# Layer A of the second chunk in other buffers, with newly searched engine orders

## The chip, the cores and the metric

One core of a Trainium2 chip runs the whole program. Its engines work side by side and wait for each other by semaphores: TensorE (PE, matmuls; its weight loads are shown as PEld), VectorE (DVE), ScalarE (ACT) and GpSimd (POOL); SyncE (SP) issues nearly all of the DMA transfers. The metric is the time of one execution in device microseconds, the median of some runs.

## The reference

Four layers are applied to x of shape 2048 x 512: A, B, A, B, each as x + layer(layernorm(x)). Both kinds have 32 heads of 16. In layer A a position sees 8 positions, two apart, back to 14; in layer B it sees the last 256.

```python
def _A_ref(x, wqkv, wo):                      # H = 32, Dh = 16, W, dil = 8, 2
    idx = pos[:, None] - off[None, :]         # off = arange(W) * dil
    logits = einsum("bhsd,bhswd->bhsw", q, k[idx]) * scale      # masked where idx < 0
    o = einsum("bhsw,bhswd->bhsd", softmax(logits), v[idx])
    return o @ wo
def _B_ref(x, wqkv, wo):
    mask = (idx[:, None] - idx[None, :] >= 0) & (idx[:, None] - idx[None, :] < 256)
    p = softmax(where(mask, einsum("bhqd,bhkd->bhqk", q, k) * Dh ** -0.5, -1e9))
    return einsum("bhqk,bhkd->bhqd", p, v) @ wo
x = x + _A_ref(_layernorm(x), A_wqkv, A_wo);  x = x + _B_ref(_layernorm(x), B_wqkv, B_wo)   # twice
```

## The kernel before

The 2048 positions are cut into 8 chunks of 256. The loop goes over the two pairs of layers and, in each, over the chunks: layer A of a chunk, then layer B of it (16 pairs; A0 and B0 are chunk 0 of the first pair, A1 and B1 chunk 1, and so on to A15 and B15). Numbers of 32 bits that go through the projections are split into a high and a low half of 16 bits ("xh" and "xl", "wB1h" and "wB1l"), and a projection does three matmuls for each block (L1015 to L1017, or L1035, L1037 and L1038).

**Preparing the weights.** `prep` loads the four weight blocks of A and then of B (s = 0, 1, 2 for q, k, v; s = 3 for the output), takes their squares to find a scale (L830, L832), writes the high halves on ACT (L911) and the low halves on DVE (L909, "wB3l", "wB1l" and so on). The blocks of q, k and v are staged in the stk tiles, which layer B later uses for its stacked q and k; their rows of padding are written by transfers (L1562, "stk<-pad") once the staged weights have been read. The output weights are staged in slots of the pool p6 (L799).

**Layer A** (`layer_a`). The norm ends with a scalar computation on DVE, POOL and DVE again (rs, L942, L945, L948); ACT scales the tile (xn, L964), makes the high half (ht, L974), and transfers transpose it (L976, L977). After the projections ACT evicts q (L1131), k and v (L1133). Each chunk needs the last 14 columns of k and v of the chunk before, the halo: POOL copies them to a spare tile (ha, L1140) and into the next chunk's k and v (L1123). Then 16 products of q with shifted k (pr, L1152, on DVE or POOL) are summed on PE (L1160); a softmax on DVE and ACT follows (max L1183, subtraction L1186); its weights are spread on PE (L1229), multiplied with shifted v on DVE (pw, L1242) and summed on POOL (L1249 to L1251) or DVE (L1247). `finish` splits the output (oh L1059, ol L1061), projects it and adds it to the residual (y, L1069), and stores it (L1080).

**Layer B** (`layer_b`). The norm scales the tile on ACT (xn, L986), transposes it on PE (L990), and splits it (xh L995, xl L996). K and Q are projected and evicted as halves (eh L1270, el L1273), written to DRAM (the puts, "re<-eh", "re<-el", L1283) and read back stacked (the stacks, "stk<-re", L1294). The scores are computed once for their maxima (L1336, L1339; DVE L1350 in a first chunk, L1354 and L1358 in the others), the maxima go through DRAM into the stacked q (L1391, L1397), then the scores come again with the maximum subtracted (L1430, L1432), the exponential on ACT (p, L1436), the mask on POOL (L1445), and the product with v (L1462), evicted to os (L1498). The output is gathered into oc, divided and finished like layer A's.

**The pools that the change touches.** po4 has one slot for each of its tags q, oa and ob; pos has two slots "os"; p6 has three. Layer B's output oc is an ob, its evictions are the two os, its exponentials p are p6. Layer A has its q and output in po4's q and oa, and its k and v in two "kv" slots; only layer A of chunk 1 in the first pair is kept elsewhere, since at that time chunk 0 still holds those slots:

```python
if l == 0 and c == 1:
    q, o = (buf("pos", [P, 4, C], F32, "os", f"{n}{l}_{c}") for n in "qo")
    kv = {s: buf("pp6", [P, 4, HALO + C], F32, "p6", f"kv{l}_{c}_{s}") for s in (1, 2)}
```

**The order of the work.** Every step is a task of a plan: `plan.add` names its engine, an assumed duration, what it reads and writes, and for a transfer a size, from which the plan assumes its time. The table ORDER holds a number for each task, by scope (A1, B0, pB for preparing B's weights, W for 110 groups of three idle matmuls that keep PE busy). On each engine the tasks run in the order of their numbers; a negative number sends a task to its other engine (for example a product from DVE to POOL). `Plan.order` then merges the five lists into the order in which the program is written, by the assumed durations and by the slots that are free; the engines themselves wait only for data and slots.

Of the kernel before, what the change touches and what calls it, by code (L numbers as in the profile page):

```python
# [678 lines left out]
def kernel(  # L679
# [420 lines left out]
    def layer_a(l, c):  # L1100
# [119 lines left out]
        for n in range(4):  # L1220
# [11 lines left out]
            for a in range(2):  # L1232
# [21 lines left out]
                plan.add("POOL", 2.56, total, r=[vpw], w=[vr], alt=("DVE", 1.84))  # L1254
        finish(l, c, o, vo)


    def layer_b(l, c):
        d = st8[l, c] = {}
        first = c == 0  # L1260
# [353 lines left out]
```

## Time and profile before

| | us |
|---|---|
| median of 3 runs | 1444.02 |
| lowest, highest | 1441.65, 1450.58 |
| the profiled execution's own time | 1450.06 |
| its span, from the first to the last instruction | 1448.3 |

The profile is of one execution. Its page gives the busy time of each engine and the span in 40 slices of about 36.2 us; the timeline gives each instruction's start, duration, engine, source line, output and inputs, and in brackets how long its engine sat idle before it and what ended that. A stretch of the busy-time view gives, after the stretch's length, the busy time of PE, PEld, DVE, ACT and POOL with the number of instructions in parentheses, then the granted clock of TensorE, the share of the DMA engines that was busy, and GB/s. A row of the waits gives the engine and line that waited, what it waited for, the total in us, how many times, and the longest.

### The profile page before, as it was taken

To read this page: it belongs to the slowest core of one execution; us is meant where nothing else is said; L and a number is where in the kernel's file an instruction comes from. 1 tells how busy PE (TensorE), PEld (TensorE's weight loads), DVE (VectorE), ACT (ScalarE), POOL (GpSimd) and SP (SyncE) were. 2 spreads that over 40 slices of the span, in tenths; PEclk is the share of its full clock that TensorE was granted. 3 is DMA by queue.
4 is the path that set the end of the run, shared out by engine and by line. 5 is a ranking of instruction groups with operands and counts; after the bars stand their busy time and mean duration, and the time that the engine had idled before them with its cause. 6 is when DMAs were issued, how large, how long until landed. Compare 5 with 4: busy or idle time off the path is not lost.

```text
span 1448.3 us, 35229 instructions
## 1 busy us (share of the span) xinstructions
PE 1340.7 (93%) x13918; PEld 782.8 (54%) x13918; DVE 1170.6 (81%) x2254; ACT 732.9 (51%) x1054; POOL 690.3 (48%) x784
## 2 busy tenths in 40 slices
PE   9985989999999998999999898999989999898998
PEld 7651646556364554736456363645637465464554
DVE  7867696996969879697996869698796978969693
ACT  6621345554555455455555434555455555545564
POOL 3445163462846336273563727254272734637232
PEclk9995989999999999999999999999999999999999
DMA  8242223233252323324133233324334242332331
GB/s 244 70 103 58 84 56 117 71 92 97 74 121 75 89 79 87 105 69 112 48 106 106 73 117 76 107 60 99 89 83 119 48 119 54 86 102 73 99 80 53
DMA packets 135943, 130.45 MB, mean 90 GB/s; under 512 B 68448, under 2 KB 94560, under 8 KB 135776
## 3 DMA queue, kind: packets, MB, share of 16 engines
q1 hardware_dynamic: 135520, 127.93, 32.7%
q8 instruction: 109, 1.79, 0.5%
q14 instruction: 58, 0.48, 0.1%
q10 hardware_dynamic: 256, 0.26, 0.1%
HBM read 67.11 MB, written 43.48 MB: 76 GB/s over the span
## 4 chain that ended last, share of the span: by engine, by line
PE 37%; DVE 17%; DMA 5%; issue 4%; SPq 3%; ACT 3%; POOL 2%; DVEq 0%; POOLq 0%; ACTq 0%
PE banks L1015 6%; PE banks L1016 5%; PE banks L1017 5%; PE banks L1462 4%; DVE m L1354 4%; DVE banks L1358 3%; PE banks L1430 3%; PE banks L1160 3%; DVE pw L1242 2%; PE banks L1037 2%; PE banks L1336 2%; PE banks L1035 2%; ACT p L1436 2%; PE banks L1038 2%; PE banks L1339 1%
## 5 line engine op out<-in xcount | busy, mean ns | idle before, releaser
L1436 ACT ACTIVATE p<-banks,sclB 128x768 f32<-128x768 f32 x480 | 418.5, 901 | 290.0 <-PE banks L1432 205.5
L1445 POOL TENSOR_SCALAR_AFFINE_SELECT p<-p 128x1024 f32<-128x1024 f32 x240 | 261.2, 1095 | 344.8 <-ACT p L1436 301.4
L1354 DVE TENSOR_REDUCE m<-banks 128x2 f32<-128x512 f32 x448 | 297.1, 685 | 3.4
L1358 DVE COPY_PREDICATED banks<-maskt,banks 128x256 f32<-128x256 int16 x448 | 179.1, 422 | 67.9 <-PE banks L1339 53.3
L1462 PE MATMUL banks<-p,v 128*32 128x128 f32 (+1 forms) x3840 | 196.8, 333 | 5.8 <-POOL p L1445 4.3
L1152 DVE TENSOR_TENSOR pr<-kv,q 128x512 f32<-128x512 f32 x220 | 153.6, 747 | 32.5 <-PE banks L1160 20.1
L1430 PE MATMUL banks<-stk,stk 64*128 64x256 f16 x960 | 136.3, 285 | 30.4 <-DVE m L1354 12.5
L1462 PEld LDWEIGHTS banks<-p,v 128*32 128x32 f32 x3840 | 106.5, 110 | 101.2 <-issue 34.3
L1242 DVE TENSOR_TENSOR pw<-banks,kv 128x1024 f32<-128x1024 f32 x128 | 152.7, 1214 | 4.2 <-POOL o L1251 2.4
L1339 PE MATMUL banks<-stk,stk 48*128 48x128 f16 (+1 forms) x1024 | 127.3, 252 | 13.1 <-DVE m L1350 9.0
L1249 POOL TENSOR_TENSOR pw<-pw 128x512 f32<-128x512 f32 x100 | 127.2, 1272 | 12.8 <-DVE pw L1242 12.6
L1336 PE MATMUL banks<-stk,stk 48*128 48x128 f16 (+1 forms) x896 | 112.0, 253 | 22.5 <-DVE m L1354 7.9
L1430 PEld LDWEIGHTS <-stk 64*128 64x128 f16 x960 | 57.0, 95 | 117.1 <-issue 108.8
L1432 PE MATMUL banks<-stk,stk 64*128 64x128 f16 x960 | 109.4, 224 | 0.0
L1336 PEld LDWEIGHTS <-stk 48*128 48x128 f16 x896 | 51.1, 95 | 98.1 <-issue 88.5
L1273 DVE SCALAR_TENSOR_TENSOR el<-banks,eh 128x512 f16<-128x512 f32 x64 | 42.4, 684 | 75.1 <-ACT eh L1270 27.4
L1270 ACT ACTIVATE eh<-banks 128x512 f16<-128x512 f32 x64 | 37.3, 596 | 77.8 <-PE banks L1017 42.3
L1250 POOL TENSOR_TENSOR pw<-pw 128x256 f32<-128x256 f32 x100 | 72.8, 728 | 7.8
L1152 POOL TENSOR_TENSOR pr<-kv,q 128x512 f32<-128x512 f32 x36 | 46.2, 1299 | 60.0 <-PE banks L1160 35.5
L1015 PE MATMUL banks<-xh,wA0h 128*128 128x256 f16 x256 | 70.1, 274 | 4.8 <-DMA xh<-ht 1.8
L1160 PE MATMUL banks<-pr,sel 128*32 128x512 f32 x512 | 71.7, 610 | 1.2 <-DVE pr L1152 1.2
L1339 PEld LDWEIGHTS <-stk 48*128 48x128 f16 x1024 | 52.8, 96 | 34.8 <-issue 32.6
(196 smaller groups left out, 3127.8 us busy)
## 6 DMA issues: line engine op xcount, KB each, us to landing
stk<-re SPq DMA_DIRECT2D x256, 96.0 KB
re<-eh SPq DMA_DIRECT2D x128, 128.0 KB
xm<-y SPq DMA_DIRECT2D x32, 256.0 KB
re<-el SPq DMA_DIRECT2D x64, 128.0 KB
y<-xm SPq DMA_DIRECT2D x32, 256.0 KB
oc<-os SPq DMA_DIRECT2D x120, 64.0 KB
os<-scr SPq DMA_DIRECT2D x15, 512.0 KB
x<-in_A_x_dram SPq DMA_DIRECT2D x16, 256.0 KB
```

The source lines that it names most:

```text
L1015: nc.tensor.matmul(ps[mp].t[:, i], wh, xh, start=k == 0, stop=False)
L1152: E.tensor_mul(pr.t, window(kv[1].t, m, 64 * tq, 64)[:, 0], qb)
L1242: nc.vector.tensor_mul(pw.t, pb.t.unsqueeze(1).broadcast_to([P, 2, W, 64]), v)
L1249: E.tensor_add(t[:, :, 0:4], t[:, :, 0:4], t[:, :, 4:8])
L1336: nc.tensor.matmul(ps.t[:, par, 0 : (2 - qb) * P], lhs, stk[hf, bef][r, col, qb * P :], start=True, stop=True)
L1339: nc.tensor.matmul(ps.t[:, par, (2 - qb) * P : 3 * P], lhs, stk[hf, now][r, col, : (1 + qb) * P], start=True, stop=True)
L1354: nc.vector.tensor_reduce(out=m.t[:, :, u, qb], in_=ps.t[:, :, 0 : 2 * P], op=ALU.max, axis=AX.X)
L1358: nc.vector.copy_predicated(t[:, :, 0:P], maskt[:, 0:P].bitcast(I16).unsqueeze(1).broadcast_to([P, 2, P]), t[:, :, 2 * P : 3 * P])
L1430: nc.tensor.matmul(o[:, two], k[:, jf * P : (jf + 1) * P], q, start=True, stop=True)
L1436: nc.scalar.activation(pt.t[:, :, 2 * i : 2 * i + 2].rearrange("p s m q -> p m s q"), ps.t[:, :, : 3 * P].rearrange("p m (s q) -> p m s q" ...
L1445: nc.gpsimd.affine_select(out=v, in_=v, pattern=[[0, 8], [-1 if b == 0 else 1, P]], compare_op=ALU.is_gt if b == 0 else ALU.is_ge, fill=0. ...
L1462: nc.tensor.matmul(o, v[:, jj, 17 * h : 17 * h + 32], rhs, start=z == 0 and (b == 0 or first), stop=z == 1 and b == 1, tile_position=(0, 3 ...
```

## The change

Three things change in the code, and all of ORDER.

The buffers of layer A, chunk 1 of the first pair: q goes to po4's q, the output to po4's ob, k and v to the two os slots. For this the os tiles are made 14 columns longer in each of their four rows, and layer B reaches the part that it uses through a flat view.

```diff
-            q, o = (buf("pos", [P, 4, C], F32, "os", f"{n}{l}_{c}") for n in "qo")
-            kv = {s: buf("pp6", [P, 4, HALO + C], F32, "p6", f"kv{l}_{c}_{s}") for s in (1, 2)}
+            q, o = buf("po4", [P, 4, C], F32, "q", f"q{l}_{c}"), buf("po4", [P, 4, C], F32, "ob", f"o{l}_{c}")
+            kv = {s: buf("pos", [P, 4, HALO + C], F32, "os", f"kv{l}_{c}_{s}") for s in (1, 2)}
...
+    def flat(b):
+        return b.t.rearrange("p g t -> p (g t)")[:, 0 : 4 * C]
...
-            os_[hf] = buf("pos", [P, 4, C], F32, "os", f"os{l}_{c}_{hf}")
+            os_[hf] = buf("pos", [P, 4, HALO + C], F32, "os", f"os{l}_{c}_{hf}")
...
-                nc.scalar.copy(os_[hf].t[:, 2 * hp : 2 * hp + 2], acc.t)
+                nc.scalar.copy(flat(os_[hf]).rearrange("p (g t) -> p g t", g=4)[:, 2 * hp : 2 * hp + 2], acc.t)
```

The other uses of the os tiles (`divide`, `leave`, `gather`, `gather_o`, `spread` and the last multiplication) go through `flat` in the same way.

What the plan assumes of some transfers:

```diff
-                    plan.add("SP", 0.5, lambda j=j, load=load: load(j), w=touched[j], size=512)
+                    plan.add("SP", 0.5, lambda j=j, load=load: load(j), w=touched[j], size=700)
...
-        plan.add("SP", 0.37, lambda: nc.sync.dma_start(xb.t, fetch(t)), r=[after[t]] if after else [], w=[vx], size=300)
+        plan.add("SP", 0.37, lambda: nc.sync.dma_start(xb.t, fetch(t)), r=[after[t]] if after else [], w=[vx], size=350)
...
-                    plan.add("SP", 0.62, put, r=ve[n], w=[vre[par][z]], size=128)
+                    plan.add("SP", 0.64, put, r=ve[n], w=[vre[par][z]], size=128)
...
-                plan.add("SP", 1.23, stack, r=vre[0] + vre[1], w=[vst[hf, i, hp]], size=192)
+                plan.add("SP", 1.3, stack, r=vre[0] + vre[1], w=[vst[hf, i, hp]], size=192)
```

And a new number for every task in ORDER, of which this is the part of scope A1 that holds chunk 1's 16 products (entries 77 to 80, 82 to 85, 87 to 90 and 92 to 95):

```diff
-        188, 191, 192, 54, 56, 22, 37, -27, 101, -26, 98, 217, -32, -30, -29, 111, 241, 116, -34, -33, 115, 245, 117,
-        -37, -36, -35, 255, 122, 123, 68, 125, 126, 127, 69, -40, 262, 138, 42, 134, 40, 263, 136, 41, 135, -140,
+        176, 182, 55, 52, 22, 20, 98, -24, 96, -28, 200, 102, 108, 113, -29, 235, 118, 117, 119, -33, 245, 122, 123,
+        121, 120, 250, 124, 125, 67, 127, 129, 131, 69, -34, 261, 144, 36, 139, 34, 262, 141, 35, 143, -147, 265,
```

Sorted by the new numbers, the engines run the following where the orders around the first layer B differ most (chunk 0 unless chunk 1 is named; j is the half of a weight block):

| | before | after |
|---|---|---|
| DVE, from the last part of layer A to layer B's norm | wB1l (j 0), ol, wB0l (j 1), residual y of tile 0, norm statistics of tile 0, y of tile 1, scale, wB3l (j 1), wB1l (j 1), wB2l (j 1), rest of the norm | wB1l (j 0), ol, wB0l (j 1), wB2l (j 1), both residuals, the whole norm, a scale and one product of chunk 1, wB1l (j 1); wB3l (j 1) after the xl of layer B |
| POOL, up to the norm's rstd (L945) | chunk 0's last sum of layer A; halo into chunk 1's v; spare halo of chunk 1's k; rstd | last sum; spare halo of chunk 1's v; halo into chunk 2's v; spare halo of chunk 1's k; one product of chunk 1; spare halo of chunk 0's v; halo into chunk 1's v; rstd |
| ACT, from the second oh to layer B's first xn | oh, one half of chunk 1's v, xn | oh, other half of v, two weight splits, first half of v, xn |
| PE, chunk 1's v projection | partly after chunk 0's output projection | done among chunk 0's output projection |
| PE, layer B | K, one product sum of chunk 1, Q, V | one product sum of chunk 1, K, one step of V, Q, V |
| SP, ahead of layer B's K puts | pads, a store of y, ht transpose, x load, second store, pads | pads, a store of y, x load, ht transpose, pad, y load, second ht transpose, pads |
| DVE, layer B's first maxima | four of them, then chunk 1's max and subtraction | chunk 1's max and subtraction, then the first of them |
| DVE / POOL, chunk 1's products | 6 / 10 | 12 / 4 |
| DVE / POOL, all products of layers A | 220 / 36 | 235 / 21 |

The number of tasks on each engine: POOL 562 before and 547 after, DVE 2021 and 2032, ACT 1040 and 1044, SP 784 and PE 3560 in both.

More of the change, by code (lines that the diff above doesn't have):

```diff
@@ L1477, in divide @@
                     v = sh.t.rearrange("p (b x) -> p b x", x=32)
-                    r = os_[hf].t[:, 2 * hp : 2 * hp + 2].rearrange("p g t -> p (g t)")
+                    r = flat(os_[hf])[:, 2 * hp * C : 2 * (hp + 1) * C]
                     nc.vector.transpose(sh.t, acc.t.rearrange("p a t -> p (a t)"))
@@ L1484, in leave @@
                 def leave(m0, E, hp=hp, hf=hf):
-                    s_ = os_[hf].t[:, 2 * hp : 2 * hp + 2].rearrange("p g t -> p (g t)")
+                    s_ = flat(os_[hf])[:, 2 * hp * C : 2 * (hp + 1) * C]
                     o_ = o.t[:, 2 * hp : 2 * hp + 2].rearrange("p g t -> p (g t)")
@@ L1510, in gather @@
             def gather(hf=hf):
-                s_ = os_[hf].t.rearrange("p g t -> p (g t)")
+                s_ = flat(os_[hf])
                 for m in range(4):
@@ L1516, in gather_o @@
             def gather_o(hf=hf):
-                s_ = os_[hf].t.rearrange("p g t -> p (g t)")
+                s_ = flat(os_[hf])
                 for m in range(4):
@@ L1528, in spread @@
         def spread():
-            nc.sync.dma_start(os_[1].t.rearrange("p g t -> p (g t)"), scr.t.unsqueeze(0).broadcast_to([16, 8, 4 * C]))
+            nc.sync.dma_start(flat(os_[1]), scr.t.unsqueeze(0).broadcast_to([16, 8, 4 * C]))
         plan.add("SP", 0.55, spread, r=[vscr, *vog], w=[vbc], size=840)
@@ L1536, in layer_b @@
             sl = slice(t * P, (t + 1) * P)
-            plan.add("DVE", 0.61, lambda E, sl=sl: E.tensor_tensor(out=o.t[:, :, sl], in0=o.t[:, :, sl], in1=os_[1].t[:, :, sl], op=ALU.mult),
+            plan.add("DVE", 0.61, lambda E, sl=sl: E.tensor_tensor(out=o.t[:, :, sl], in0=o.t[:, :, sl], in1=flat(os_[1]).rearrange("p (g t) -> p g t", g=4)[:, :, sl], op=ALU.mult),
                      r=[vbc, *vog], w=[v], mode="S", alt=("POOL", 1.3))
```

834 rows, old and new, of the table ORDER are left out of this document.

## The prediction

> **What bounds the kernel now.** I read the page first, then the busy time by stretches, then each engine's timeline over the first 130 us, because the buffers that the change moves are used only there.
>
> ```profile
> span 1448.3 us, 35229 instructions
> ...
> PE 1340.7 (93%) x13918; PEld 782.8 (54%) x13918; DVE 1170.6 (81%) x2254; ACT 732.9 (51%) x1054; POOL 690.3 (48%) x784
> ...
> PE   9985989999999998999999898999989999898998
> ...
> PEclk9995989999999999999999999999999999999999
> ```
>
> TensorE (PE) is busy 93% of the span and VectorE (DVE) 81%. The weak places are slices 3 and 4 (80 to 150 us), where both the PE digits and the clock fall, and some later slices with an 8, such as 23 and 25 (796 to 833 and 869 to 905 us).
>
> ```profile
> 75.00:112.00 37.00, 27.66 (x197) 17.46 (x195) 21.72 (x33) 8.68 (x14) 16.90 (x18) 0.94 0.47 112
> 112.00:150.00 38.00, 25.40 (x140) 7.89 (x140) 33.08 (x104) 6.98 (x11) 20.31 (x24) 0.61 0.19 46
> 150.00:280.00 130.00, 124.45 (x1287) 77.34 (x1286) 103.97 (x220) 63.13 (x93) 50.44 (x58) 0.96 0.32 89
> 280.00:1400.00 1120.00, 1053.67 (x11269) 608.87 (x11267) 926.37 (x1737) 582.20 (x835) 559.47 (x617) 0.97 0.33 88
> ```
>
> From 280 to 1400 us PE is busy 1053.67 of 1120 us: 66.3 us idle, 6%. What is gained before 280 us therefore moves the end by about as much, for everything behind it is PE work that only begins earlier. From 75 to 112 us no engine is full (PE 27.66 of 37, DVE 21.72): a chain of latencies sets the pace. From 112 to 150 us DVE is the bound (33.08 of 38) and the clock is down to 0.61.
>
> **The change part by part.** *The buffers.* Before, layer A of chunk 1 kept k and v in two of the three p6 slots, two of which first hold the staged B output weights.
>
> ```profile
> 77.32 0.70 POOL L1123 COPY kv<-ha 128x56 f32<-128x56 f32 x1 [8.10 <-DVE wB3l L909]
> ...
> 80.98 0.70 POOL L945 TENSOR_TENSOR rs<-rs,mhalf 128x2 f32<-128x2 f32 x1 [2.29 <-DVE rs L942]
> 81.63 0.23 POOL L1123 COPY kv<-ha 128x56 f32<-128x56 f32 x1
> ```
> ```profile
> 64.95 1.12 ACT L911 ACTIVATE wB2h<-stk,pscB 128x1024 f16<-128x1024 f32 x1
> ...
> 71.23 0.60 ACT L1059 CAST oh<-o 128x512 f16<-128x512 f32 x1
> 77.37 0.60 ACT L1133 ACTIVATE kv<-banks 128x512 f32<-128x512 f32 x1 [5.54 <-DVE wB3l L909]
> 81.91 0.81 ACT L986 ACTIVATE xn<-y,rs 128x512 f32<-128x512 f32 x1 [3.94 <-DVE rs L948]
> ...
> 86.03 0.81 ACT L964 ACTIVATE xn<-x,rs 128x512 f32<-128x512 f32 x1
> ...
> 98.58 0.60 ACT L1270 ACTIVATE eh<-banks 128x512 f16<-128x512 f32 x1 [0.39 <-PE banks L1017]
> ...
> 149.56 0.59 ACT L1498 COPY os<-banks 128x512 f32<-128x512 f32 x1 [2.88 <-PE banks L1462]
> ```
>
> GpSimd (POOL) stood 8.10 us before it could write chunk 1's halo, ScalarE (ACT) 5.54 us before it could evict v: both ended by "wB3l", the last read of a staged slot. With k and v in the os slots, which layer B of chunk 0 doesn't fill before its first eviction at 149.56 us, this wait is gone. By itself that is worth nothing on the chain: right after, POOL waits for "DVE rs" until 80.98 and ACT for "DVE rs" until 81.91. Late next is DVE. The other side of the exchange, q in po4's q slot and the output in ob, should wait for nobody: chunk 0's products have long read their q when chunk 1's is evicted, and layer B's own output enters ob only behind that eviction at 149.56.
>
> *DVE's order around the norm of layer B, chunk 0.* This is what the freed slot allows.
>
> ```profile
> 73.82 0.74 DVE L1069 SCALAR_TENSOR_TENSOR y<-banks,sclA,y 128x512 f32<-128x512 f32 x1
> ...
> 75.21 0.73 DVE L1069 SCALAR_TENSOR_TENSOR y<-banks,sclA,y 128x512 f32<-128x512 f32 x1
> ...
> 75.98 1.28 DVE L909 SCALAR_TENSOR_TENSOR wB3l<-stageB,pscB,wB3h 128x1024 f16<-128x1024 f32 x1
> 77.17 1.47 DVE L909 SCALAR_TENSOR_TENSOR wB1l<-stk,pscB,wB1h 128x512 f16<-128x512 f32 x2
> 78.52 1.28 DVE L909 SCALAR_TENSOR_TENSOR wB2l<-stk,pscB,wB2h 128x1024 f16<-128x1024 f32 x1
> ...
> 80.72 0.17 DVE L942 TENSOR_SCALAR rs<-mv 128x2 f32<-128x2 f32 x1
> ```
>
> Before, between the last residual (75.21) and the first norm scalars (80.72) lie wB3l (75.98 to 77.17, 1.19), wB1l (77.17 to 78.52, 1.35), a scale (0.12) and wB2l (1.19). wB3l had to be early, since a slot hung on it. The new numbers put wB3l, wB1l and the scale behind the scalars and wB2l before the first residual. wB2l still counts; the rest is 1.19 + 1.35 + 0.12 = 2.66 us. So the scalars come at about 78.06, and xn on ACT at 79.25 where it was 81.91. On POOL the rstd now has six instructions ahead of it: two halo pairs, a spare halo copy and one product, 5 x 0.23 (the row at 81.63; one at 77.32 took 0.70) and a product of about 1.3 (its row is below), together 2.4 us. They wait for v's last eviction, which ACT does after the second oh (71.23 + 0.60), one other eviction (0.60) and two weight splits (1.12 each), so it ends near 75.3; POOL is free near 77.7, 0.6 us before it's wanted (78.06 + 0.26, as 80.98 stood to 80.72).
>
> *Behind the norm.* PE gets chunk 1's first product sum ahead of K instead of between K and Q, which is neutral for Q, and one step of V (two matmuls, 98.38 to 98.81) ahead of Q:
>
> ```profile
> 98.38 0.38 PE L1037 MATMUL banks<-wB2h,xh 128*128 128x512 f16 x1
> ...
> 98.81 0.38 PE L1035 MATMUL banks<-wB2h,xl 128*128 128x512 f16 x1
> ```
>
> That is +0.43. Q's last high half was evicted at 98.58; it comes 2.66 - 0.43 = 2.2 us earlier. SyncE's queue (SP) gets two transfers moved ahead of the K puts, a transposed ht tile and a y load:
>
> ```profile
> 82.06 1.26 SPq L976 DMA_TRANSPOSE xh<-ht  x1
> 84.71 0.36 SPq L1088 DMA_DIRECT2D x<-in_A_x_dram  x1
> ...
> 88.68 2.54 SPq L1562 DMA_DIRECT2D stk<-pad  x4
> 93.19 2.53 SPq L1283 DMA_DIRECT2D re<-eh  x4
> ...
> 103.39 5.67 SPq L1294 DMA_DIRECT2D stk<-re  x8
> ```
>
> They issue in 1.26 and 0.36 us. The y load also needs a free x slot, which the xn of chunk 2's second tile gives (86.03 + 0.81, now some 2.7 earlier: 84.2), before the pads can go anyway. Queued behind them are the pads of stk and all puts. SP stood idle from 91.22 (88.68 + 2.54) to 93.19, 1.97 us, which hides 1.62; with that cover gone they'd cost 1.6. The stacks then issue near 101.2 instead of 103.39.
>
> *The stretch bound by DVE.*
>
> ```profile
> 112.41 0.42 DVE L1350 CUSTOM_DVE_ANT_0 j<-banks,maskt 128x256 bf16<-128x256 f32 x1 [6.15 <-DMA stk<-pad]
> ...
> 116.04 0.69 DVE L1183 TENSOR_REDUCE mx<-banks 128x64 f32<-128x512 f32 x1
> 116.76 0.69 DVE L1186 TENSOR_TENSOR e<-banks,mx 128x512 f32<-128x512 f32 x1
> ```
>
> Chunk 1's max and subtraction (0.69 each, 1.4 us) stood among layer B's maxima. In the new order they stand ahead of the first of these, in the wait for the stacks (the bracket at 112.41: DVE idle 6.15 us). To be ready in time, chunk 1's products go from 6 on DVE and 10 on POOL to 12 and 4. That takes 1.4 us out of a stretch where DVE is the bound.
>
> *The products elsewhere.* Over the whole kernel 15 more products are on DVE (220 to 235, POOL 36 to 21), 9 of them outside chunk 1.
>
> ```profile
> L1152 DVE TENSOR_TENSOR pr<-kv,q 128x512 f32<-128x512 f32 x220 | 153.6, 747 | 32.5 <-PE banks L1160 20.1 <-ACT q L1131 8.9 <-ACT kv L1133 3.2
> ...
> L1152 POOL TENSOR_TENSOR pr<-kv,q 128x512 f32<-128x512 f32 x36 | 46.2, 1299 | 60.0 <-PE banks L1160 35.5 <-ACT q L1131 16.7 <-ACT kv L1133 5.9
> ```
> ```profile
> 86.78 0.68 DVE L1152 TENSOR_TENSOR pr<-kv,q 128x512 f32<-128x512 f32 x1
> ```
>
> At 0.68 each that is 6.1 us of DVE, where from 280 to 1400 us it has 194 us idle (1120 - 926.37). I take 0, since PE is the one that is full; 6.1 is the upper end. As to a gain: the 220 products took 153.6 us instead of 220 x 0.68 = 149.6, so all collisions with POOL cost 4.0, and 15 of 36 POOL products fewer save at most 1.7. The Trainium skill has a rule for this, on its page "SBUF — State Buffer", section "Who interferes with whom": a DVE operation with two SBUF inputs and a GpSimd operation that reads SBUF exclude each other for the whole instruction. By that rule each product that leaves POOL could free its whole stay there, 15 x (1.30 - 0.68) = 9.3 us, and the sum would be 9.3 lower; the trace's 4.0 us for all collisions says that few of them meet.
>
> *The orders of the rest.* Every list is new. PE's changes between kinds of matmul, counted in both lists, are 1172 before and 1201 after, +29. The trace shows no price for one. Nearest are
>
> ```profile
> PEld L1430 <- issue: 108.8, 285, 1.9
> ```
>
> 0.38 us of idle weight loading at an entry into layer B's scores, so 11.1 us as the upper end; and PE's own 66.3 us idle over the 907 changes that fall to 280 to 1400 us by share (1172 x 1120/1448), 0.07 each, 2.0 us. I take 2.0, because PE's weight loads overlap its matmuls. Below nothing is possible too: new orders may fill the holes where DVE and POOL are both full:
>
> ```profile
> 800.00:820.00 20.00, 16.77 (x142) 6.35 (x138) 18.23 (x54) 8.34 (x13) 17.44 (x21) 0.85 0.30 64
> ...
> 880.00:900.00 20.00, 15.09 (x143) 6.20 (x142) 19.42 (x32) 8.79 (x14) 19.06 (x24) 0.83 0.31 70
> ```
>
> PE idles 3.2 and 4.9 us of 20 there, 8.1 together. The longer sizes given to the first loads only steer the search; no instruction changes with them.
>
> Sum: -2.2 - 1.4 + 2.0 = -1.6 us. The profiled execution took 1450.06 us with a span of 1448.3; the median of the runs is 1444.02. So 1448.5 for such an execution, and 1442.4 for the median.
>
> **The rivals.** *The start gives nothing.* POOL's six instructions ahead of rstd wait for v, and SP's two transfers stand ahead of the puts. From 0.6 us of lateness of v's eviction the norm slips one for one; at 3.3 (2.66 + 0.6) it stands where it stood. Against it: PE finishes chunk 1's v in the new order before layer A's last output matmuls. Then -1.4 + 2.0: 1444.6.
>
> *The rest gets slower.* The 29 changes of kind lie mostly between 280 and 1400 us, where PE is the bound, and each costs the full 0.38: 1444.02 - 3.6 + 11.1 = 1451.5. From 3.6/29 = 0.12 us each the kernel is slower than before; from 0.62 on by over 1% (14.4 us, about what a measurement can tell from no change). For it: the row of weight loads as it stands. Against: 0.07 by PE's own idle time.
>
> *The holes are filled.* With 4.9 + 3.2 us regained and no cost of the changes: 1444.02 - 3.6 - 8.1 = 1432.3. For it: fewer slow products on POOL. Against: in these slices DVE is itself 97% busy (19.42 of 20), and the products went to DVE. A mechanism of its own would end near here: if each POOL product holds DVE off for its whole 1.30 us, the 15 free 9.3 us, and the time is 1444.02 - 3.6 - 9.3 = 1431.1; the 4.0 us above speak against it. This is the rule on SBUF named above.
>
> **How the numbers follow.** Forecast 0.45 (own range 1438 to 1447), start gives nothing 0.15, rest slower 0.22, holes filled 0.15, products that exclude each other 0.03. Under 1429.6, faster by over 1%, lies the far part of these last two, with some more holes filled: 0.11. Over 1458.4, slower by over 1%, lies the far part of the slower rival, with DVE's 6.1 us on top of the 11.1: 1457.6 and beyond, 0.09. Within 1%: 0.80. The range goes from 1430 (the holes and the products' 1.7 us: 1430.6) to 1457 (the slower rival with nearly all of DVE's 6.1 us).
>
> **What would show it.** In the changed profile POOL's halo write shows no "wB3l" any more; the norm's scalars of layer B, chunk 0 start 2 to 3 us earlier than 80.72, the K puts at about 91, the stacks at about 101.2; no max of chunk 1 stands among layer B's first maxima, and DVE is idle less between 102 and 112 us. PE's busy time from 280 us to the end, and its idle time there (66.3 of 1120), say whether the rest was even. The prediction is wrong if the norm doesn't move, if PE's idle time in the rest grows by more than 6 us, or if the holes close.

## The result, and the profile after

The changed kernel took 1440.72 us, the median of 20 runs (1434.69 to 1446.66); 20 runs of the kernel before, made beside them, had a median of 1448.11 us (1441.38 to 1452.15). The ratio is 0.9957, with a 95% interval of 0.9941 to 0.9973: 6.2 us less. The profiled execution took 1440.79 us, its span 1439.1 us. The forecast was 1442.4 us, in the case "within 1%". It was counted from 1444.02 us, the median of the first 3 of the 20 runs of before, which is 4.1 us under the median of all 20.

The page of the changed kernel, in the same lines as before:

```profile
span 1439.1 us, 35171 instructions
...
PE 1339.7 (93%) x13918; PEld 783.0 (54%) x13918; DVE 1172.9 (82%) x2265; ACT 736.9 (51%) x1058; POOL 675.0 (47%) x769
...
PE   9975999999999999999999898998999999999997
...
PEclk9995989999999999999999999999999999999999
```

PE's busy time is the same (1340.7 before, 1339.7 now) and the span 9.2 us shorter: what went is idle time. The busy time by stretches, in the columns explained for the kernel before:

```profile
75.00:112.00 37.00, 25.25 (x172) 15.20 (x173) 24.84 (x40) 8.21 (x13) 7.99 (x10) 0.85 0.52 128
112.00:150.00 38.00, 26.68 (x156) 10.13 (x156) 33.56 (x113) 7.34 (x12) 20.77 (x24) 0.65 0.14 38
150.00:280.00 130.00, 124.41 (x1282) 76.47 (x1285) 102.81 (x212) 63.82 (x94) 53.31 (x60) 0.96 0.31 85
280.00:1400.00 1120.00, 1060.34 (x11357) 611.26 (x11356) 931.70 (x1756) 587.91 (x842) 550.00 (x608) 0.97 0.34 89
```

From 280 to 1400 us PE idles 59.7 us (1120 - 1060.34), where it idled 66.3: in these two executions the rest became better, not 2.0 us worse. How much of the 6.6 us is the scatter of single executions is taken up behind the experiments. From 75 to 112 us DVE does more (24.84 us, before 21.72), yet the stretch behind it is still DVE's, 33.56 of 38 us. The timelines of the engines show why so little of the start arrived there. First DVE:

```profile
76.92 0.17 DVE L942 TENSOR_SCALAR rs<-mv 128x2 f32<-128x2 f32 x1
...
104.60 0.69 DVE L1183 TENSOR_REDUCE mx<-banks 128x64 f32<-128x512 f32 x1 [1.17 <-PE banks L1160]
105.32 0.69 DVE L1186 TENSOR_TENSOR e<-banks,mx 128x512 f32<-128x512 f32 x1
112.14 0.42 DVE L1353 CUSTOM_DVE_ANT_0 j<-banks,maskt 128x256 bf16<-128x256 f32 x1 [6.12 <-DMA stk<-pad]
```

Then POOL, SP and PE, each from its own timeline:

```profile
73.48 0.76 POOL L1140 COPY ha<-kv 128x56 f32<-128x56 f32 x1 [4.90 <-ACT kv L1133]
...
76.09 0.23 POOL L1123 COPY kv<-ha 128x56 f32<-128x56 f32 x1
77.17 0.70 POOL L945 TENSOR_TENSOR rs<-rs,mhalf 128x2 f32<-128x2 f32 x1 [0.85 <-DVE rs L942]
```
```profile
90.56 2.54 SPq L1286 DMA_DIRECT2D re<-eh  x4
...
94.50 1.33 SPq L1565 DMA_DIRECT2D stk<-pad  x2
...
100.20 8.51 SPq L1297 DMA_DIRECT2D stk<-re  x12
108.76 1.31 SPq L1565 DMA_DIRECT2D stk<-pad  x2
```
```profile
105.06 0.27 PE L1342 MATMUL banks<-stk,stk 48*128 48x256 f16 x1 [0.20 <-DMA stk<-re]
...
112.62 0.26 PE L1342 MATMUL banks<-stk,stk 48*128 48x128 f16 x1 [6.32 <-DVE m L1353]
```

The norm's scalars start at 76.92 us where they stood at 80.72, no halo write waits for wB3l, the K puts are issued at 90.56 (before 93.19) and the stacks at 100.20 (103.39); chunk 1's max and subtraction lie ahead of layer B's maxima. Then it stops: the first of these starts at 112.14 us, before 112.41. DVE had been idle for 6.12 us, until the transfer "stk<-pad" issued at 108.76 had landed, and PE, whose first scores began at 105.06, waited 6.32 us for that max. A max neither reads nor writes stk or pad. But the instruction for the first chunk also has an output that nobody reads, and the code puts it into a tile with the tag "junk" of a pool with one slot, the same tag and slot as the pad tile from which that transfer reads:

```python
junk = pools["ps1"][0].tile([P, 3 * P], BF16, tag="junk", name=f"j{l}_{c}")
...
pad = buf("ps1", [P, 3 * P], BF16, "junk", f"pad{some[0]}")
```

So the first max had to wait until the last pad was read. The plan doesn't know of this, since the tile is made inside the instruction's function and isn't in its lists. In the kernel before the same row stands in the prediction (112.41, 6.15 us, "stk<-pad"); I read its bracket as a wait for the stacks.

### The profile page after: what moved, and what is told of

Same layout as the page of the kernel before. It is cut to its first block, busy times and chain, and to the rows that moved or that the text cites. A ratio compares the mean times of both kernels' runs of the same rounds, so it can differ in the third digit from the quotient of the medians.

```text
span 1439.1 us, 35171 instructions
## 1 busy us (share of the span) xinstructions
PE 1339.7 (93%) x13918; PEld 783.0 (54%) x13918; DVE 1172.9 (82%) x2265; ACT 736.9 (51%) x1058; POOL 675.0 (47%) x769
## 4 chain that ended last, share of the span: by engine, by line
PE 53%; DVE 19%; POOL 8%; issue 6%; DMA 5%; ACT 4%; SPq 4%; DVEq 0%; POOLq 0%; ACTq 0%
PE banks L1015 8%; PE banks L1017 7%; PE banks L1016 7%; PE banks L1465 6%; DVE m L1357 4%; PE banks L1037 3%; PE banks L1433 3%; POOL pw L1249 3%; PE banks L1160 3%; DVE banks L1361 3%; PE banks L1035 3%; PE banks L1038 3%; DVE pw L1242 3%; PE banks L1339 3%; ACT p L1439 2%
## 5 line engine op out<-in xcount | busy, mean ns | idle before, releaser
L1152 DVE TENSOR_TENSOR pr<-kv,q 128x512 f32<-128x512 f32 x235 | 156.5, 716 | 24.4 <-PE banks L1160 18.3
L1242 DVE TENSOR_TENSOR pw<-banks,kv 128x1024 f32<-128x1024 f32 x128 | 153.0, 1212 | 4.1 <-POOL o L1251 2.3
L1342 PE MATMUL banks<-stk,stk 48*128 48x128 f16 (+1 forms) x1024 | 128.8, 250 | 13.9 <-DVE m L1353 10.3
L1339 PE MATMUL banks<-stk,stk 48*128 48x128 f16 (+1 forms) x896 | 113.3, 252 | 17.3 <-DVE m L1357 5.9
L1339 PEld LDWEIGHTS <-stk 48*128 48x128 f16 x896 | 50.2, 94 | 95.3 <-issue 86.7
L1015 PE MATMUL banks<-xh,wA1h 128*128 128x256 f16 x256 | 71.3, 278 | 0.7 <-DVE pw L1242 0.7
L1017 PE MATMUL banks<-xh,wA1l 128*128 128x256 f16 x256 | 71.1, 278 | 0.0
L1016 PE MATMUL banks<-xl,wA1h 128*128 128x256 f16 x256 | 71.1, 278 | 0.0
```

Of the source, the lines that this page charges most:

```text
L1015: nc.tensor.matmul(ps[mp].t[:, i], wh, xh, start=k == 0, stop=False)
L1016: nc.tensor.matmul(ps[mp].t[:, i], wh, xl, start=False, stop=False)
L1017: nc.tensor.matmul(ps[mp].t[:, i], wl, xh, start=False, stop=k == 3)
L1242: nc.vector.tensor_mul(pw.t, pb.t.unsqueeze(1).broadcast_to([P, 2, W, 64]), v)
L1339: nc.tensor.matmul(ps.t[:, par, 0 : (2 - qb) * P], lhs, stk[hf, bef][r, col, qb * P :], start=True, stop=True)
L1342: nc.tensor.matmul(ps.t[:, par, (2 - qb) * P : 3 * P], lhs, stk[hf, now][r, col, : (1 + qb) * P], start=True, stop=True)
```

## The experiments

Each ratio is from five rounds against the kernel before on the same chip, with its 95% interval. Where ORDER was written in fewer lines, the lines of the code are 21 lower (L924 is L945, L1318 is L1339); code lines behind `flat` are 3 higher than in the kernel before.

The milestones of the first layer B in the trace of each, in us. "First pw" is DVE's first weighted product of chunk 0 (L1242), the norm is the row L942, the first spread is SP's first transfer os<-scr (L1532), with which chunk 0's layer B gets its divisors:

| kernel | code, start order | first pw | norm | stacks | first max | first spread | ratio |
|---|---|---|---|---|---|---|---|
| before | old, old | 53.83 | 80.72 | 103.39 | 112.41 | 215.60 | 1 |
| before again (e5) | old, old | 54.25 | 81.15 | 104.72 | 113.74 | 216.54 | |
| sizes (e9) | old, old | 55.85 | 82.75 | 107.10 | 116.97 | 220.37 | 1.003 |
| wide os (e6) | wide os, old | 55.00 | 81.88 | 105.34 | 114.94 | 218.48 | 1.0025 |
| buffers (e1) | new, old | 55.56 | 82.47 | 105.97 | 115.28 | 218.54 | 1.004 |
| new rest (e3) | new, old | 55.27 | 82.17 | 105.30 | 114.81 | 218.20 | 1.0059 |
| new rest later (e10) | new, old | 54.53 | 81.43 | 104.55 | 114.18 | 217.64 | 0.9987 |
| own scratch before (e7) | old, old | 56.09 | 82.98 | 106.84 | 111.90 | 214.87 | 0.9965 |
| after | new, new | 53.16 | 76.92 | 100.20 | 112.14 | 212.26 | 0.9957 |
| after again (e8) | new, new | 53.46 | 77.21 | 101.26 | 112.82 | 215.08 | 0.9959 |
| new start (e2) | new, new | 52.85 | 76.63 | 100.08 | 111.66 | 212.75 | 1.0007 |
| products back (e11) | new, new | 52.85 | 76.62 | 100.37 | 112.36 | 212.91 | 0.9983 |
| old sizes (e12) | new, new | 53.75 | 77.51 | 100.82 | 112.43 | 212.85 | 0.9987 |
| own scratch after (e4) | new, new | 53.25 | 77.03 | 100.98 | 106.71 | 207.16 | 0.9935 |

**The buffers alone (e1).** The changed code with the old table; as one line of it:

```diff
-    "S": [0, 1, 4, 7],
+    "S": [6, 5, 1, 2],
...
```

> The new buffers, with every number of ORDER as it was before. Theory (the orders carry the gain, the buffers only allow them): POOL's halo write of chunk 1 no longer waits 8.10 us for wB3l, POOL and ACT stand waiting later instead, the norm scalars of layer B, chunk 0 stay at about 80.7 us, and the time is that of the kernel before, ratio 0.999 to 1.001. Rival (the freed slots themselves help): the K puts or layer B's first max come earlier and the ratio is near 0.996, that of the whole change.

Measured: 1.004 (1.0025 to 1.0055), 5.8 us slower. POOL's timeline of this kernel:

```profile
70.92 0.23 POOL L1102 COPY kv<-ha 128x56 f32<-128x56 f32 x1
...
82.72 0.71 POOL L924 TENSOR_TENSOR rs<-rs,mhalf 128x2 f32<-128x2 f32 x1 [11.41 <-DVE rs L921]
```

The halo is written at 70.92, before 77.32 with a wait of 8.10 us; POOL then waits 11.41 us for the norm instead. So the slots came free and nobody gained, as forecast; but neither theory had a loss.

**What the loss is (e6, e9).** Of the three parts of the code, e6 keeps the wider os tiles and the plan's longer sizes, e9 the sizes alone:

```diff
-                    plan.add("SP", 0.5, lambda j=j, load=load: load(j), w=touched[j], size=512)
+                    plan.add("SP", 0.5, lambda j=j, load=load: load(j), w=touched[j], size=700)
...
```

> The kernel before with only the os tiles made 14 columns longer per row, the flat view, and the plan's longer sizes; q, the output, k and v of chunk 1 where they were, old ORDER. Tells what makes the new buffers with the old ORDER 0.4% slower (1.004, 1.0025 to 1.0055). If the layout of the memory or the assumed sizes do it: 1.003 to 1.005 again. If it is the move of the four buffers: 0.999 to 1.001.

> The kernel before with only the plan's longer sizes for four kinds of transfer: no instruction changes, and on each engine the order is the old one, but the plan merges the five lists otherwise and so gives 430 of 5618 uses of the accumulator banks another bank. Tells what made the wider os tiles with the longer sizes 0.25% slower (1.0025, 1.001 to 1.0041). If the banks do it: 1.002 to 1.004. If the layout of the memory does it: 0.999 to 1.001. My prediction took these sizes as free: 1.0.

Measured: 1.0025 (1.001 to 1.0041) and 1.003 (1.0014 to 1.0045). The sizes alone cost as much as the rest of the code with them, though each engine runs the same instructions in the old order. What differs is the accumulator bank that 430 of 5618 uses get; every other tile takes its slot in the order of before. The plan deals e6 exactly the banks of e9, and e1 the same but for three uses, so the banks are what the three slower kernels share. (The order in which the five lists are merged into one program also differs; no run separates it from the banks.) PE's waits from 280 to 1400 us, the kernel before (again, e5) and then e9, show it:

```profile
PE banks L1430 <- DVE m L1354: 10.2, 20, 1.5
PE banks L1336 <- DVE m L1354: 7.5, 17, 1.0
...
PE banks L1336 <- ACT p L1436: 2.1, 6, 0.5
```
```profile
PE banks L1430 <- DVE m L1354: 12.2, 23, 1.5
PE banks L1336 <- DVE m L1354: 8.4, 20, 1.4
PE banks L1336 <- ACT p L1436: 7.0, 11, 1.6
```

Layer B's scores (L1336) now wait 7.0 us for exponentials "p" of another group to leave their bank, before 2.1. The other traces agree: this row has 2.9 and 2.6 us in the two others with the old banks (before, e7) and 5.3 us in both e6 and e1. With the two rows of maxima it's 27.6 us against 19.8; there the old banks have 22.1 and 20.3, the others 25.3 and 23.6. The Trainium skill, on its page "Perfetto Trace Analysis", section "Matmuls", says that independent groups of matmuls should rotate through the banks, so that the reading out of one lies beside the matmuls of the next; this trace agrees, since scores waited for the readers of their banks, 4.9 us longer in that row with 430 other banks.

**The sizes within the change (e12).** The changed kernel with the four sizes put back:

```diff
-                    plan.add("SP", 0.5, lambda j=j, load=load: load(j), w=touched[j], size=700)
+                    plan.add("SP", 0.5, lambda j=j, load=load: load(j), w=touched[j], size=512)
...
```

> The changed kernel with only the plan's four sizes put back to the old ones: the same instructions in the same order on each engine, 301 uses of the accumulator banks in another bank. With the old ORDER the longer sizes cost 0.3% (1.003, 1.0014 to 1.0045). If an order suits the sizes under which it was found: 0.997 to 1.000, that is 2 to 6 us slower than the changed kernel (0.9957 and 0.9959). If the longer sizes are worse in themselves: 0.991 to 0.994. If it is a matter of which tasks happen to share a bank, and here they are harmless: 0.995 to 0.9965.

Measured: 0.9987 (0.9972 to 1.0003). Here the old sizes are the worse ones, by 0.3%; its interval and that of the change (0.9941 to 0.9973) only just touch. So neither set is better in itself: as the expectation had it, an order goes with the banks that the plan dealt out while it was searched. Where the 0.3% arises e12's trace doesn't show: PE idles 59.3 us from 280 to 1400 us, in the changed kernel 59.7.

**The start and the rest (e2, e3, e10).** All have the changed code; on each engine the plan's first tasks run in the one order and all others behind them in the other. Their tables differ from the changed one in hundreds of numbers, of which these are scope S, the first, in e3 and e10, and eight entries of A15, the last layer A, in e2:

```diff
-    "S": [0, 1, 4, 7],
+    "S": [6, 5, 1, 2],
...
-1818, 1815, 1819, 3174, 1826, 1827, 1823, 1824
+1810, 1811, 1812, 3173, -501, 1818, 1819, 1820
...
```

> The new order for the 991 tasks that the plan starts in the first 200 us, the order of before for all others. Theory (about 3.3 us are won at the start and kept to the end, the rest of the 7 to 9 us late in the kernel): ratio 0.9975 to 0.998, 3 to 3.6 us less than before. Rival A (the start is swallowed, because layer B's first max comes only 0.3 us earlier in both traces): 0 to 0.5 us less, ratio 0.9997 to 1. Rival B (the start carries all): ratio 0.995 to 0.996.

> The reverse: the order of before for the 945 tasks of the first 200 us, the new one for all others, with its additional changes between kinds of matmul. Theory (both parts win): 3 to 4 us less, ratio 0.997 to 0.998. My prediction's own step (each additional change costs PE 0.07 us): 2 us more, ratio 1.001. Rival (the start carries all): ratio 1.0.

> The changed code, the order of before for the 1510 tasks of the plan's first 300 us and the new one behind. In the earlier form with the cut at 200 us, 92.0 us lay between the first two broadcasts of layer B's divisors instead of 84 to 85: 7 us lost where two orders meet, so it said nothing of the rest. Theory (the new orders of the rest win 3 to 5 us from 300 us on, beside what the code alone costs, 1.004): ratio 1.0005 to 1.002 and 1136 to 1142 us from the second broadcast to the end. Rival (only the start wins): 1.004. My prediction's step (2 us lost to more changes between kinds of matmul): 1.005.

Measured: 1.0007 (0.9992 to 1.0022), 1.0059 (1.0041 to 1.0078) and 0.9987 (0.9967 to 1.0008). SP's timelines of e3 and e10 show the first two spreads:

```profile
218.20 0.55 SPq L1511 DMA_DIRECT2D os<-scr  x1
...
310.24 0.54 SPq L1511 DMA_DIRECT2D os<-scr  x1
```
```profile
217.64 0.55 SPq L1511 DMA_DIRECT2D os<-scr  x1
...
301.82 0.54 SPq L1511 DMA_DIRECT2D os<-scr  x1
```

In e3 92.0 us lie between them, in e10 84.2: e3's cut broke the order where two meet, and its ratio says nothing of the rest. From the second spread to the end e10 takes 1137.6 us, as expected, but that proves nothing: the kernel before takes 1148.3 us there in its first trace and 1136.3 us in e5. What shows a gain of the rest are the ratios of e10 and e1, whose intervals don't meet. Against the code with the old table (1.004) the new start is worth 1.0007/1.004, 4.8 us, and the new rest 0.9987/1.004, 7.6 us. Together with the 5.8 us of the code this is 6.6 us less, and the change measured 6.2. The intervals are each about 2 to 3 us wide to either side, the cuts lie at 200 and at 300 us, and each deals out other banks too, so the split is no finer than that.

**The changed kernel again (e8).** Unchanged, beside e6 and e7:

> The changed kernel, unchanged, on the same chip as the three runs beside it. The parts did not add up: buffers alone 1.004, new start 1.0007, new rest 1.0059, all of it 0.9957. Theory (the new orders of start and rest only pay together, since each was searched for the buffers and for what lies before it): 0.994 to 0.997 again. Rival (the 0.9957 was the chip's): 0.998 to 1.001.

Measured: 0.9959 (0.9944 to 0.9974).

**A tile of its own for the unused output (e4, e7).** In the changed kernel and in the one before:

```diff
-                            junk = pools["ps1"][0].tile([P, 3 * P], BF16, tag="junk", name=f"j{l}_{c}")
+                            junk = pools["ps1"][0].tile([P, 3 * P], BF16, tag="junk2", name=f"j{l}_{c}")
```

> The changed kernel, in which the unused output of layer B's first maxima goes to a tile of its own instead of the slot that the last pad transfer reads from. Theory (that shared slot swallowed most of the earlier start): the first max no longer waits for the pad transfer and starts near 106.3 instead of 112.14 us, PE's wait of 6.3 us for it goes, DVE's work of the stretch to 150 us starts 5 to 6 us earlier, and the kernel is 4 to 6 us faster than the changed one: ratio to the kernel before 0.991 to 0.993. Rival A (the stacks land too late as well): the first max comes at 108 to 110 and the ratio is 0.994 to 0.995. Rival B (another wait takes its place before 150 us, p's first products or mput): the first max comes early and the time stays, 0.9955 to 0.996.

> The kernel before with only the unused output of layer B's first maxima in a tile of its own. Theory (the shared slot holds both kernels back at the same place, the changed one more, since its stacks are issued 3.2 us earlier): the first max starts near 109.5 instead of 112.41 us, and the kernel is 2.5 to 3.5 us faster, ratio 0.9975 to 0.998. Rival A (it matters only where the stacks come early): 1.0. Rival B (the wait is worth as much here as in the changed kernel): ratio 0.9955 to 0.9965.

Measured: e4 0.9935 (0.991 to 0.996), e7 0.9965 (0.9953 to 0.9978). DVE's timeline of e4, then SP's, then DVE's of e7:

```profile
105.38 0.69 DVE L1183 TENSOR_REDUCE mx<-banks 128x64 f32<-128x512 f32 x1 [1.17 <-PE banks L1160]
106.10 0.69 DVE L1186 TENSOR_TENSOR e<-banks,mx 128x512 f32<-128x512 f32 x1
106.71 0.41 DVE L1353 CUSTOM_DVE_ANT_0 j<-banks,maskt 128x256 bf16<-128x256 f32 x1
```
```profile
100.98 8.20 SPq L1297 DMA_DIRECT2D stk<-re  x12
109.23 1.31 SPq L1565 DMA_DIRECT2D stk<-pad  x2
```
```profile
111.90 0.42 DVE L1350 CUSTOM_DVE_ANT_0 j<-banks,maskt 128x256 bf16<-128x256 f32 x1 [2.18 <-PE banks L1339]
```

In e4 the first max follows the subtraction without a wait, 2.5 us before the last pad is even issued; in e7 it waits 2.18 us, for PE's scores. The shared slot is shown as the cause in both. By the first spread e4 is 6.0 us ahead of the five kernels with the same start (207.16 against a mean of 213.17). By the runs it is about 3 us faster than the changed kernel, less than the 4 to 6 us I expected, and the two intervals overlap; it is the fastest version here. In e7 the 5.0 us were more than the 2.5 to 3.5 I expected, though 3.5 lies within its interval: the wait was worth no less before the change than after.

**The head (e5).** The kernel before once more, for a profile:

> The kernel before, unchanged, for a profile from the chip of the next three runs. In the two kernels that keep the old order at the start (the new buffers alone, and the new order for the rest) the load of x that VectorE waits for at 20 us in the profile of before landed 1.5 to 1.75 us later. Theory (a load lands when the memory of that chip and execution lets it): VectorE's wait for it varies here too, anywhere between 1.3 and 2.6 us. Rival (the new buffers delay it): it is 1.33 us again, and layer B's first max is at 112.4.

DVE's wait for the load of x near 20 us, from its timelines in e5, e1, e7 and the changed kernel:

```profile
20.88 0.69 DVE L936 BATCH_NORM_STATS2 b<-x 128x6 f32<-128x512 f32 x1 [1.81 <-DMA x<-in_A_x_dram]
```
```profile
22.03 0.69 DVE L915 BATCH_NORM_STATS2 b<-x 128x6 f32<-128x512 f32 x1 [2.61 <-DMA x<-in_A_x_dram]
```
```profile
22.11 0.69 DVE L936 BATCH_NORM_STATS2 b<-x 128x6 f32<-128x512 f32 x1 [0.87 <-DMA x<-in_A_x_dram]
```
```profile
25.40 0.69 DVE L936 BATCH_NORM_STATS2 b<-x 128x6 f32<-128x512 f32 x1 [0.31 <-DMA x<-in_A_x_dram]
```

With the old order of loads the wait is 0.87 to 2.61 us, the extremes in kernels with the old and with the new buffers, and DVE's first pw comes at 53.83 to 56.09 us, mean 55.05 over eight traces. With the new order of loads the wait is at most 0.54 us, and the first pw comes at 52.85 to 53.75, mean 53.22 over six. It isn't this load alone: in e7, where its wait is the shortest, DVE had already waited 2.56 us for its first weights (before, 1.38), and the first pw is the latest, 56.09. The new table changes every engine's order in the head, and no run changes that of the loads alone.

**The products (e11).** 18 products of layers A on POOL again, from A5 on; entries 76 to 83 of A5, where a negative number means POOL:

```diff
-158, 577, 581, 580, 579, 1020, 588, 586
+160, 577, 579, -153, -152, 1020, 586, 584
...
```

> The changed kernel with 18 products of layers A, from 414 us on, moved back from VectorE to GpSimd, each where the plan had it in time. My prediction took the move of 15 as worth nothing. If so: ratio to the kernel before 0.9945 to 0.997, as the changed kernel (0.9957 and 0.9959). Rival A (a product on GpSimd costs its 1.30 us where PE waits for the sum): each adds up to 0.6 us, 3 to 11 us more, ratio 0.998 to 1.003. Rival B (VectorE is the bound in the full slices): each saves up to 0.68 us, ratio 0.988 to 0.993.

Measured: 0.9983 (0.9967 to 0.9998), 3.7 us slower than the changed kernel. The groups of products, of the changed kernel and of e11:

```profile
L1152 DVE TENSOR_TENSOR pr<-kv,q 128x512 f32<-128x512 f32 x235 | 156.5, 716 | 24.4 <-PE banks L1160 18.3 <-ACT kv L1133 2.9 <-ACT q L1131 2.8
...
L1152 POOL TENSOR_TENSOR pr<-kv,q 128x512 f32<-128x512 f32 x21 | 25.5, 1224 | 60.6 <-PE banks L1160 42.0 <-ACT q L1131 16.0 <-ACT kv L1133 2.7
```
```profile
L1131 DVE TENSOR_TENSOR pr<-kv,q 128x512 f32<-128x512 f32 x217 | 153.2, 755 | 27.8 <-PE banks L1139 21.6 <-ACT q L1110 3.2 <-ACT kv L1112 2.7
...
L1131 POOL TENSOR_TENSOR pr<-kv,q 128x512 f32<-128x512 f32 x39 | 50.6, 1312 | 76.4 <-PE banks L1139 54.0 <-ACT q L1110 16.0 <-ACT kv L1112 6.5
```

18 products left DVE, and its time for products fell by 3.3 us, not by 18 x 0.68 = 12.2. Take DVE's busy time for products as a x (its own) + c x (POOL's): 153.6 = 220a + 36c before and 156.5 = 235a + 21c after give a = 0.627 and c = 0.434. For e11 that makes 217 x 0.627 + 39 x 0.434 = 153.0 us, and 153.2 were measured. But 0.43 us is no price of a product on POOL: in e10 (231 and 25) the same sum gives 155.7 us and 153.6 were measured, in e2 (225 and 31) 154.6 and 156.0. It depends on how many meet, and the timelines show what happens then. Two rows of DVE and one of POOL in the changed kernel:

```profile
77.91 1.13 DVE L948 SCALAR_TENSOR_TENSOR rs<-mv,rs 128x2 f32<-128x2 f32 x1 [0.70 <-POOL rs L945]
...
85.05 1.30 DVE L1152 TENSOR_TENSOR pr<-kv,q 128x512 f32<-128x512 f32 x1
```
```profile
77.84 1.19 POOL L1152 TENSOR_TENSOR pr<-kv,q 128x512 f32<-128x512 f32 x1
```

This POOL product ends at 79.03, and DVE's tiny norm step, 0.16 us before the change, ends at 79.04. POOL's next product begins at 84.63, takes 1.18 us and ends at 85.81, and DVE's product that began beside it ends at 86.35. DVE's instruction is held until POOL's is over. Taken one by one over all 14 traces, a DVE product that meets no POOL instruction lasts at most 0.69 us; the 258 that last longer than 0.72 us, up to 1.69 us, each end 0.54 to 0.55 us after a POOL instruction that had begun before them, a product or a mask (p<-p). Before, 22 of the 220 are held, together 13.9 us beyond 0.68 each; after the change 14 of the 235, 7.7 us; in e11 24 of the 217, 15.5 us. How much of the 3.7 us comes from that, and how much from the 173 uses that get another bank here, is open.

## Why the prediction was right, and where its steps were wrong

The time was forecast 1.7 us too high and the case was right. That it came so near is partly luck: of the change itself, 6.2 us by the ratio and 7.4 between the medians, the sum had only 1.6, and a base that was 4.1 us low made up for most of what it lacked. Of the steps:

*The buffers by themselves are worth nothing*: right. The halo's wait went and another took its place (e1), and what e1 lost the sizes lose alone (e9).

*2.66 us earlier at the norm*: right, a little more. Over eight traces with the old start and six with the new the norm comes at 81.94 and 76.99 us, 4.95 earlier, of which 1.83 are the head's; 3.1 us remain. POOL was free at 76.3 (76.09 + 0.23) and wanted at 77.17, so "the start gives nothing" fell with its condition. Not foreseen was that the next POOL product would hold DVE's last norm step (the rows at 77.84 and 77.91): xn on ACT begins at 79.08, near the forecast 79.25, and would have begun about 1.0 us earlier. SP's idle time hid the two transfers, as costed.

*The head*: not in the sum. I compared the orders only around the first layer B; the new ones of the head are worth 1.8 us at the first pw, and the trace of before (53.83) was the best of its eight and hid most of it.

*The wait for the stacks* ahead of layer B's first max: this reading failed. The bracket named stk<-pad, the transfer behind the first eight stacks, and I added chunk 1's max and subtraction into a wait that the stacks were to end. Of the 4.8 us by which the stacks come earlier (means 105.40 and 100.62) the first max got 2.3 (114.62 to 112.28, without e4 and e7). The start still yields 4.7 us at the first spread (217.91 to 213.17): with the 1.4 us for chunk 1's max and subtraction, taken as costed, that leaves 1.0 us that I have not traced.

*The sizes change no instruction and so nothing*: the step that was mis-sized most. They deal out other banks, 0.3% with either order (e9, e12). The change with the old sizes is at 0.9987, 1.9 us less (its interval reaches 1.0), near the forecast 1.6; the sizes made 6.2 of it.

*29 more changes between kinds of matmul, +2.0*: wrong in sign, as a term for the rest. PE's waits from 280 to 1400 us, of before and after:

```profile
PE banks L1430 <- DVE m L1354: 11.3, 22, 1.5
PE banks L1336 <- DVE m L1354: 7.9, 16, 1.4
```
```profile
PE banks L1433 <- DVE m L1357: 8.0, 17, 1.0
...
PE banks L1339 <- DVE m L1357: 5.9, 11, 1.3
```

Its waits for layer B's maxima fell from 19.2 to 13.9 us, 5.3 of the 6.6 us of idle time that went. That is the largest difference of three pairs of traces with the same orders: e5 and e8 show 17.7 to 14.6 us in these rows and 62.3 to 57.7 us of idle time, e7 and e4 17.7 to 16.2, and 61.6 to 62.6. So the rows fell by 1.5 to 5.3 us, and by the traces alone what the rest won as a whole is known only to a few us. If a change of kind has a price, it is smaller than what the order won; the rival with 0.38 us each is out.

*The holes*: not filled. PE idles 3.2 and 4.3 us in the same two windows of the changed kernel, before 3.2 and 4.9 (the work in them begins some us earlier now):

```profile
800.00:820.00 20.00, 16.83 (x124) 5.98 (x114) 17.62 (x58) 6.75 (x10) 15.82 (x19) 0.86 0.38 94
880.00:900.00 20.00, 15.74 (x143) 6.24 (x135) 19.64 (x33) 9.48 (x14) 19.06 (x23) 0.83 0.32 78
```

*The products, taken as 0*: the base was wrong. A product in a row of its own shows 0.68 us, but four in a row on DVE take 2.50, while POOL does nothing:

```profile
100.00:112.00 12.00, 5.20 (x29) 1.42 (x26) 3.88 (x6) 1.80 (x3) 0.00 (x0) 0.83 0.53 140
```
```profile
100.93 2.50 DVE L1152 TENSOR_TENSOR pr<-kv,q 128x512 f32<-128x512 f32 x4 [0.93 <-PE banks L1160]
```

So the 4.0 us for all collisions were too few: 153.6 us is the time in which DVE was busy with any product, and in it neighbours overlap by some 0.07 us, while 0.68 us is one product by itself. By themselves the 220 take 747 ns in the mean, and the collisions, counted one by one, cost 13.9 us. Moving 15 products saved DVE 6.2 us of being held (13.9 to 7.7) and cost it 15 x 0.625 = 9.4 us of work, near the measured 2.9 us net (153.6 to 156.5); it took 20.7 us from POOL. The rule of the Trainium skill that the prediction weighed, on "SBUF — State Buffer", section "Who interferes with whom", agrees with each of these meetings. What the rival of 9.3 us had wrong is how many there are: before, the 36 products on POOL held 15 of DVE's, and masks held 7.

## What to carry to other kernels

Read the name in a wait's bracket literally: when an instruction waits for a transfer whose data it doesn't use, look for a buffer that the two share, scratch outputs first. Where a planner also deals out banks and slots, an edit that changes no instruction still changes what waits for what, so take it apart from the rest with a run of its own. Take the price of an instruction from several in a row, not from one with its tail, and the price of a collision from the instructions that met, one by one. Before you credit a stretch with a gain, look at the same stretch in a second execution of the same kernel.

## What was not expected of the hardware

A VectorE instruction that reads two tiles in SBUF was held until a GpSimd product or mask that had begun before it was over, even where it was a norm step of 128 x 2 elements (1.13 us instead of 0.16). It goes the other way too: a GpSimd product took 1.17 to 1.20 us, but 1.58 to 1.71 us in 9 of 36 cases before, each ending 1.03 to 1.05 us after a VectorE product that had begun before it. In the first 20 us the loads that VectorE waits for land with a scatter of about 2 us from one execution to the next (first pw within 2.26 us over eight traces); with the new orders of the start the first pw stays within 0.90 us over six.
